# Filler matmuls and a new division of filter copies and products in the first-sequence prologue of a fused FFT-filter and SwiGLU kernel

## The chip, the cores and the metric

One core of one Trainium2 chip. Times are device microseconds (us) of one execution; a profiled execution also has a span, which is 1.8 us shorter than its time (about 2.0 in two kernels). "Clock" is the granted tensor-engine clock as a share of full speed. In the profile's views PE is the tensor engine, PEld its weight loads, DVE VectorE, ACT ScalarE, POOL GpSimd, and SP the engine whose queue issues most transfers.

## The reference

```python
def _attn_ref(x, filt_r, filt_i):            # x (8, 3008, 256), filters (1505, 256)
    X = np.fft.rfft(x, axis=1)
    Y = X * (filt_r + 1j * filt_i)[None]
    return np.fft.irfft(Y, n=x.shape[1], axis=1)

def _moe_ref(x, w_gate, w_val, w_out, rms_g):  # 24064 tokens, 256 -> 1536 -> 256
    xn = x / np.sqrt(np.mean(x * x, axis=-1, keepdims=True) + 1e-06) * rms_g
    g = xn @ w_gate
    return (g / (1 + np.exp(-g)) * (xn @ w_val)) @ w_out
```

## The kernel before

The transform of length 3008 = 47 x 64 is done as matrix products. Eight sequences pass through; the first has a path of its own (the *prologue*), because nothing can run beside it: load x, transform, transpose, multiply by the filter, transform back, transpose, norm, first gate product. From then on one long *loop* of gate, value and output products runs, and the transforms of the later sequences are woven into it.

The filter stands in memory once, but the products need it on both halves of the partitions, so a copy makes the other half. Where these copies ran, before:

```python
def f_dup(c):                       # other half of filter chunk c (4 chunks)
    for t, a, e in ((fr[c], HALF, 0), (fi[c], 0, HALF)):
        if c == 2 or (c == 3 and a):
            nc.scalar.activation(out=t[a:a + HALF], in_=t[e:e + HALF], func=AXT.Copy)
        else:
            nc.gpsimd.tensor_copy(out=t[a:a + HALF], in_=t[e:e + HALF])
```

A *unit* `b_unit(0, i)` is a pair of forward products into PSUM and two filter products (`ss` or `sg`, then `s2`) on VectorE, or, for units 4, 8 and 11, a ScalarE copy `v` out of PSUM and two products on GpSimd. The prologue from the transposes on:

```python
for i in range(8):
    t1_unit(i)                      # 8 transposes + a tile copy
f_dup(0); f_load(3, filt_i, ...); f_dup(1)
for i in range(16):
    if i == 7: f_dup(3)
    b_unit(0, i)
    if i % 2 and i >= 5:
        bit_unit(i - 5)             # inverse products, then copies into gT
        bit_unit(i - 4)
    if i == 4: f_dup(2)
    if i == 11: w_load(0); w_load(1)
...                                 # t2_unit: transposes of gT; norm; scaling
```

For sequence 1, stores and a broadcast load share the in-order SP queue, and the norm's scaling `xn_unit` sits on GpSimd in a fixed slot after the load:

```python
def g_store(b, c):
    nc.sync.dma_start(g_d[b, 4 * c:4 * c + 4, :, :]..., st[b]["t3"].pop(c))
def rho_load(b, m):                 # waits for the small store r_tmp<-rho
    nc.sync.dma_start(rb[:, 0:w], r_d[b, m, 0:w].partition_broadcast(P))
...
# steps: q_unit, rho_load, xn_unit at slots s1 + r
norm_plan(b, m, n_at[m], n_at[m] + step, (2, 6, 10) if b > 1 else (2, 5, 8))
```

## Time and profile before

| | us |
|---|---|
| median of 3 runs | 904.34 (903.84 to 907.87) |
| profiled run: time, span | 903.62, 901.8 |
| first filter product of unit 0 on VectorE | 24.69 |
| last filter product: VectorE, GpSimd | ends 43.41, 41.49 |
| last copy into gT | ends 44.75 |
| first gate output (start of the first Silu) | 52.71 |
| from there to the end ("the loop") | 849.09 |

The landmarks split the span into parts. The last two rows add up to the span. The line of the first gate output (start, duration, engine and line of the kernel, operation, and in brackets what was waited for):

```profile
52.71 0.60 ACT L436 ACTIVATE sg<-pg 128x512 f16<-128x512 f32 x1 [0.23 <-PE pg L432]
```

The other lines that carry this table are in the prediction; the important reading there is the table of stretches, where the clock is 0.67 in the middle of the prologue and 1.00 in the loop.

### The profile page before, as it was taken

Reading aid. Unit: us, or ns where it says so; the run is one execution under the profiler, and the core shown is the slowest. Engines: PE = TensorE matmul, PEld = TensorE weight load, DVE = VectorE, ACT = ScalarE, POOL = GpSimd, SP = SyncE. Lnnn points to the kernel's source line nnn. Section 1 sums busy time; section 2 is a strip of 40 time slices with the busy share of each in tenths; the row PEclk is TensorE's granted clock in tenths of the full one; section 3 lists DMA queues with packets and bytes.
Section 4 is the critical chain, followed back from the end, with each engine's and each line's share of the span. In section 5 each row is a group of like instructions: output and inputs, shape, how many; then the busy total and the mean of one; then the engine's idle time right before and its main releaser. Section 6 shows DMA issues by size and latency. Waiting matters only on the chain.

```text
span 901.8 us, 17407 instructions
## 1 busy us (share of the span) xinstructions
PE 877.6 (97%) x6244; PEld 563.8 (63%) x6244; DVE 678.5 (75%) x1088; ACT 621.4 (69%) x1060; POOL 430.1 (48%) x387
## 2 busy tenths in 40 slices
PE   7789999899999999999999999999999999999997
PEld 5665666666666666666666666666666666666556
DVE  7856767788887887888778886887878887555555
ACT  7667656677777776887667776787657765676444
POOL 6942730455535671477425672377515662145300
PEclk9699999999999999999999999999999999999999
DMA  9395634674655347444654346242262232222201
GB/s 197 71 194 162 144 75 164 155 169 87 170 152 132 68 97 198 118 95 95 141 153 98 95 103 164 95 116 83 83 176 71 66 81 60 93 65 47 72 24 48
DMA packets 79907, 100.91 MB, mean 112 GB/s; under 512 B 8128, under 2 KB 56512, under 8 KB 79436
## 3 DMA queue, kind: packets, MB, share of 16 engines
q1 hardware_dynamic: 69356, 83.32, 34.0%
q0 software_dynamic: 10384, 16.35, 11.4%
q8 instruction: 49, 0.80, 0.4%
q14 instruction: 38, 0.31, 0.1%
q10 hardware_dynamic: 80, 0.13, 0.1%
HBM read 67.67 MB, written 46.78 MB: 127 GB/s over the span
## 4 chain that ended last, share of the span: by engine, by line
PE 83%; issue 6%; DMA 5%; POOL 2%; DVE 2%; ACT 2%; SPq 0%; POOLq 0%; ACTq 0%
PE po L451 24%; PE pg L432 24%; PE pv L432 24%; PE psi L286 3%; PE psb L241 2%; DMA fr<-in_filt_r_dram 2%; PE psn L318 2%; PE psa L204 2%; DMA rb<-r_tmp 1%; DMA g_tmp<-t 1%; DVE o L458 1%; PE psq L347 1%; DVE hh L437 1%; DMA r_tmp<-rho 0%; POOL xc L189 0%
## 5 line engine op out<-in xcount | busy, mean ns | idle before, releaser
L437 DVE TENSOR_TENSOR hh<-pv,sg 128x512 f16<-128x512 f32 (+2 forms) x588 | 393.1, 669 | 200.1 <-ACT sg L436 88.8
L436 ACT ACTIVATE sg<-pg 128x512 f16<-128x512 f32 (+2 forms) x588 | 340.8, 580 | 227.3 <-PE pg L432 217.7
L451 PE MATMUL po<-wo,hh 128*128 128x256 f16 x2244 | 342.9, 272 | 2.8 <-DVE o L458 1.9
L432 PE MATMUL pg<-xn,wg 128*128 128x512 f16 (+2 forms) x1176 | 339.8, 370 | 0.0
L432 PE MATMUL pv<-xn,wv 128*128 128x512 f16 (+2 forms) x1176 | 339.7, 370 | 0.0
L451 PEld LDWEIGHTS <-hh 128*128 128x128 f16 x2256 | 216.4, 98 | 97.4 <-issue 3.8
L277 POOL TENSOR_TENSOR s<-s,s 128x512 f16<-128x512 f16 x96 | 111.0, 1156 | 225.3 <-DVE s L271 150.5
L432 PEld LDWEIGHTS <-wv 128*128 128x128 f16 x1176 | 114.9, 98 | 129.1 <-issue 0.6
L411 POOL TENSOR_TENSOR xn<-y,rb 128x1024 f16<-128x1024 f32 (+1 forms) x45 | 126.1, 2803 | 49.8 <-DMA rb<-r_tmp 36.2
L432 PEld LDWEIGHTS <-wg 128*128 128x128 f16 x1176 | 111.4, 98 | 12.6 <-issue 0.3
L353 POOL TENSOR_TENSOR rho<-u,mhalf 128x4 f32<-128x4 f32 (+1 forms) x48 | 48.9, 1019 | 71.8 <-DVE u L351 71.4
L291 ACT ACTIVATE t<-psi 96x512 f16<-96x512 f32 x112 | 66.3, 592 | 12.6 <-PE psi L286 6.4
L324 ACT ACTIVATE y<-psn,gsb 128x512 f32<-128x512 f32 (+1 forms) x94 | 63.8, 678 | 9.4 <-PE psn L318 2.3
L271 DVE TENSOR_TENSOR s<-psb,fi 64x512 f16<-64x512 f32 x96 | 65.7, 684 | 3.0
L273 DVE SCALAR_TENSOR_TENSOR s<-psb,fi 64x512 f16<-64x512 f32 x96 | 66.5, 693 | 1.3
L247 DVE TENSOR_TENSOR s<-psb,fr 128x512 f16<-128x512 f32 x96 | 65.3, 680 | 0.0
L330 ACT ACTIVATE sq<-psn 128x512 f16<-128x512 f32 (+1 forms) x94 | 54.8, 583 | 0.0
L338 POOL TENSOR_TENSOR sq<-sq 128x512 f16<-128x512 f16 (+1 forms) x34 | 38.5, 1131 | 32.8 <-ACT sq L330 32.7
L209 ACT ACTIVATE t<-psa 128x512 f16<-128x512 f32 x70 | 41.8, 597 | 5.6 <-PE psa L204 2.4
L286 PE MATMUL psi<-s,wi 128*128 128x256 f16 x248 | 45.4, 273 | 0.0
L241 PE MATMUL psb<-t,wb 96*128 96x256 f16 x224 | 43.0, 272 | 1.4 <-DVE s L264 0.9
L286 PEld LDWEIGHTS <-wi 128*128 128x128 f16 x248 | 24.3, 98 | 27.1 <-issue 2.0
(102 smaller groups left out, 544.9 us busy)
## 6 DMA issues: line engine op xcount, KB each, us to landing
out_dram<-o SPq DMA_DIRECT2D x83, 256.0 KB
xc<-in_x_dram POOLq DMA_DIRECT2D x56, 192.0 KB, 6.2
z_tmp<-t SPq DMA_DIRECT2D x28, 384.0 KB
t<-z_tmp SPq DMA_DIRECT2D x28, 384.0 KB
g_tmp<-t SPq DMA_DIRECT2D x56, 192.0 KB
rb<-r_tmp SPq DMA_DIRECT2D x41, 256.0 KB
t<-g_tmp SPq DMA_DIRECT2D x21, 384.0 KB
t<-g_tmp SPq DMA_DIRECT2D x7, 320.0 KB
```

Source lines behind the costliest of these rows:

```text
L247: nc.vector.tensor_tensor(out=s1, in0=ps, in1=f1, op=ALU.mult)
L271: nc.vector.tensor_tensor(out=s2[a], in0=ps[e], in1=f2[e], op=ALU.mult)
L273: nc.vector.scalar_tensor_tensor(out=s2[a], in0=ps[e], scalar=-1.0, in1=f2[e], op0=ALU.mult, op1=ALU.mult)
L277: nc.gpsimd.tensor_tensor(out=s, in0=s1, in1=s2, op=ALU.add)
L286: nc.tensor.matmul(ps[:, u, :], wi_at(q, 2 * i + u), ss[q][:, u, :], start=(q == 0), stop=(q == n - 1))
L291: nc.scalar.activation(out=st[b]["t3"][c][:, 2 * r:2 * r + 2, :], in_=ps[0:KR], func=AXT.Copy)
L324: nc.scalar.activation(out=y[:, dh, 0:w], in_=ps[:, 0:w], func=AXT.Identity, scale=gsb[:, dh:dh + 1])
L411: nc.gpsimd.tensor_tensor(out=xv, in0=yv, in1=rv.unsqueeze(1).to_broadcast([P, 2, n, P]), op=ALU.mult)
L432: nc.tensor.matmul(ps[:, 0:w], wt[:, dt_, ts(jt, P)], xn[:, dt_, :], start=(dt_ == 0), stop=(dt_ == 1))
L436: nc.scalar.activation(out=sg[:, 0:w], in_=pg[:, 0:w], func=AXT.Silu)
L437: nc.vector.tensor_tensor(out=hh[:, 0:w], in0=pv[:, 0:w], in1=sg[:, 0:w], op=ALU.mult)
L451: nc.tensor.matmul(po[s4 // per][:, s4 % per, :], hh[:, ts(s4, P)], wo[:, jt, :], start=(jt == 0 and s4 % per == 0), stop=(jt == JT - 1 an ...
```

## The change

Its intent is to shorten the prologue in two ways. *Fillers*: 63 matmuls on zeros, whose results nobody reads, are put where the tensor engine would wait; they are meant to keep the clock up. *Division of work*: the copies of filter halves go to ScalarE, GpSimd and one transfer; GpSimd takes four units (3, 7, 10, 13) rather than three; six of the eight transpose groups come after the forward products of units 0 to 3 instead of ahead of them, four of them between filter products; small pieces of the tail move to ScalarE.

```diff
+    def b_mm(b, i):
+        ps = bank(3 if b else (0, 3, 4, 5)[i % 4], "psb")...
+        if b == 0 and i > 3:
+            nc.tensor.matmul(ps[:, 0, :], wz[:, 0:P], wz[:, 0:D], start=True, stop=True)
...
-        if (i in (5, 8, 11, 14)) if b else (i in (4, 8, 11)):
+        if (i in (5, 8, 11, 14)) if b else (i in (3, 7, 10, 13)):
...
     def y_first(y, pss, dh):
+        if dh:
+            nc.scalar.activation(out=y[:, dh, :], in_=pss[dh], func=AXT.Identity, ...)
+            return
...
+    def keep_warm(n):
+        o = st[0]["g"][1][:, 4 * KR:512]
+        for _ in range(n):
+            nc.tensor.matmul(o, wz[:, 0:P], wz[:, 0:P], start=True, stop=True)
...
         for m in range(6):
+            if m == 4:
+                warm_up(6, 0)
...
-        for i in range(8):
-            t1_unit(i)
-        f_dup(0)
-        f_load(3, filt_i, fi[3], HALF, nc.gpsimd)
-        f_dup(1)
+        A, G, S = nc.scalar, nc.gpsimd, nc.sync
+        t1_unit(0)
+        t1_unit(1)
+        ps0 = [b_mm(0, i) for i in range(4)]
+        t1_unit(2)
+        t1_unit(3)
+        f_dup(0, 0, A)          # chunk, part (0 real, 1 imaginary), engine
+        f_dup(0, 1, G)
+        f_dup(1, 1, G)
+        f_dup(3, 0, S)
         for i in range(16):
-            if i == 7:
-                f_dup(3)
-            b_unit(0, i)
+            if i == 5:
+                f_dup(2, 1, G)
+            b_unit(0, i, ps0[i] if i < 4 else None)
+            if i == 0:
+                t1_unit(4)
+                t1_unit(5)
+            elif i == 1:
+                t1_unit(6)
+                t1_unit(7)
+            elif i == 3:
+                f_dup(1, 0, A)
+            elif i == 7:
+                f_dup(2, 0, A)
+            elif i == 10:
+                f_dup(3, 1, A)
             if i % 2 and i >= 5:
                 bit_unit(i - 5)
+                keep_warm(4)
                 bit_unit(i - 4)
-            if i == 4:
-                f_dup(2)
-            if i == 11:
+            if i == 13:
                 w_load(0)
                 w_load(1)
         for i in range(12, 16):
             bit_unit(i)
+            if i % 2 == 0:
+                keep_warm(4)
+        warm_up(2, 0)
         t2_unit(0, 1)
...
         first = n_first()
+        warm_up(4, 0)
+        y_first(*first, 1)
         q_unit(0, 0)
+        warm_up(3, 0)
         y_first(*first, 0)
         scale_split(0, 0)
-        y_first(*first, 1)
-        t2_unit(2, 1)
+        t2_unit(2, 0)
         t2_unit(3, 0)
+        warm_up(3, 0)
         scale_apply(0, 0, 3)
+        warm_up(1, 0)
```

The cuts leave out the new signatures of `f_load` and `f_dup`, other PSUM banks for the transposes, and the order of the first loads.

More of the change, by code (lines that the diff above doesn't have):

```diff
@@ L36 @@
 KC = 8
-FC = (8, 8, 8, 8)
 def _make_tables():
@@ L165 @@
     wi = glob.tile([P, 2, K2, P], FP16)
-    fr = [glob.tile([P, n, D], FP32, name="fr%d" % c) for c, n in enumerate(FC)]
-    fi = [glob.tile([P, n, D], FP32, name="fi%d" % c) for c, n in enumerate(FC)]
+    fr = [glob.tile([P, KC, D], FP32, name="fr%d" % c) for c in range(K2 // KC)]
+    fi = [glob.tile([P, KC, D], FP32, name="fi%d" % c) for c in range(K2 // KC)]
     wg = glob.tile([P, 2, DFF], FP16)
@@ L227, in wi_at @@
         return wi[:, q, k, :] if k else tb[:, 3 + q, :]
-    def b_unit(b, i):
-        if b:
-            ps = bank(3, "psb")
-        else:
-            ps = bank((0, 3, 4, 5)[i % 4], "psb")
-        ps = ps.rearrange("p (a d) -> p a d", a=2)
+    def b_mm(b, i):
+        ps = bank(3 if b else (0, 3, 4, 5)[i % 4], "psb").rearrange("p (a d) -> p a d", a=2)
+        if b == 0 and i > 3:
+            nc.tensor.matmul(ps[:, 0, :], wz[:, 0:P], wz[:, 0:D], start=True, stop=True)
         for u in range(2):
@@ L241, in b_unit @@
             nc.tensor.matmul(ps[:, u, :], w[:, k, :], t, start=True, stop=True)
+        return ps
+    def b_unit(b, i, ps=None):
+        if ps is None:
+            ps = b_mm(b, i)
         f1, f2 = filt(2 * i, 2)
@@ L379, in y_first @@
     def y_first(y, pss, dh):
+        if dh:
+            nc.scalar.activation(out=y[:, dh, :], in_=pss[dh], func=AXT.Identity, scale=gsb[:, dh:dh + 1])
+            return
         nc.vector.tensor_scalar(out=y[:, dh, :], in0=pss[dh], scalar1=gsb[:, dh:dh + 1],
@@ L483, in o_store, with f_load @@
             nc.sync.dma_start(prev[:, H - 1, :], o3[64:P, 3, :])
-    NC = K2 // KC
     def raw(src, row, ap):
         return bass.AP(tensor=src.tensor, offset=src.offset + row * D, ap=ap)
-    def f_load(c, src, t, p0, eng):
+    def f_load(c, e, eng):
         lo = 1 if c == 0 else 0
+        src, t, p0 = ((filt_r, fr[c], 0), (filt_i, fi[c], HALF))[e]
         eng.dma_start(t[p0 + 16:p0 + 63:2, :, :].rearrange("p a d -> p (a d)"),
@@ L500, in f_load, with f_dup @@
             eng.dma_start(t[p0 + 1:p0 + 48:2, 0, :], raw(src, 32, [[64 * D, 24], [1, D]]))
-    def f_dup(c):
-        for t, a, e in ((fr[c], HALF, 0), (fi[c], 0, HALF)):
-            if c == 2 or (c == 3 and a):
-                nc.scalar.activation(out=t[a:a + HALF], in_=t[e:e + HALF], func=AXT.Copy)
-            else:
-                nc.gpsimd.tensor_copy(out=t[a:a + HALF], in_=t[e:e + HALF])
+    def f_dup(c, e, eng):
+        t = (fr, fi)[e][c]
+        a, o = (0, HALF) if e else (HALF, 0)
+        if eng is nc.scalar:
+            eng.activation(out=t[a:a + HALF], in_=t[o:o + HALF], func=AXT.Copy)
+        elif eng is nc.sync:
+            eng.dma_start(t[a:a + HALF], t[o:o + HALF])
+        else:
+            eng.tensor_copy(out=t[a:a + HALF], in_=t[o:o + HALF])
     def at_unit(m, dh):
@@ L528, in t1_unit @@
         st[0]["t2"][g] = dst
-        pool, tag = ((psO, "po0"), (psO, "po1"), (psM, "mx"), (psB, "mb"))[g % 4]
+        pool, tag = ((psG, "pg"), (psV, "pv"))[g % 2]
         ps = pool.tile([P, 4, D], FP16, tag=tag, name="pt1")
@@ L536, in t1_unit @@
                 nc.tensor.transpose(ps[:, a, ts(dh, P)], src, ident)
-        if g % 2 == 0 or g == 7:
+        if g not in (1, 4):
             nc.vector.tensor_copy(out=dst, in_=ps[0:KR])
@@ L626 @@
         nc.sync.dma_start(wbp, tab["wbp"])
-        for c in range(NXC):
-            x_load(0, c)
         def zero(t):
@@ L632, in zero @@
                                  in_=mhalf[0:HALF, 0:1].to_broadcast([HALF, KC * D]), func=AXT.Copy, scale=0.0)
+        for c in range(NXC):
+            x_load(0, c)
         nc.gpsimd.memset(fr[0][0:HALF], 0.0)
@@ L642 @@
             zero(fi[c][HALF:P])
-        for c in range(4):
-            f_load(c, filt_r, fr[c], 0, nc.sync)
-            if c < 3:
-                f_load(c, filt_i, fi[c], HALF, nc.gpsimd)
         with nc.allow_non_contiguous_dma(reason="one gain a partition"):
             nc.sync.dma_start(gsb, moe_rms_g.rearrange("(a p) -> p a", p=P))
+        for c in range(4):
+            f_load(c, 0, nc.sync)
+            f_load(c, 1, nc.gpsimd if c < 3 else nc.sync)
         warm_up(14, 1)
```

## The prediction

> **What bounds the kernel now.** I read the page's busy shares first, then busy time by stretch to see where the tensor engine is not full, then the chain that ended last from 0 to 56 us, and last the vector engine's and GpSimd's timelines of that part.
>
> ```profile
> PE 877.6 (97%) x6244; PEld 563.8 (63%) x6244; DVE 678.5 (75%) x1088; ACT 621.4 (69%) x1060; POOL 430.1 (48%) x387
> ```
>
> ```profile
> 0.00:23.90 23.90, 19.20 (x219) 13.82 (x220) 17.04 (x27) 18.18 (x22) 16.43 (x27) 0.93 0.89 195
> 23.90:44.60 20.70, 15.70 (x161) 12.12 (x159) 17.29 (x29) 13.56 (x22) 19.42 (x18) 0.67 0.32 63
> 44.60:52.70 8.10, 6.08 (x53) 4.26 (x54) 4.01 (x10) 3.36 (x6) 5.74 (x9) 0.80 1.21 176
> 52.70:901.80 849.10, 836.66 (x5813) 533.63 (x5811) 640.16 (x1024) 586.25 (x1011) 388.53 (x336) 1.00 0.44 110
> ```
>
> The columns are stretch, length, then busy us (and instructions) of PE, PEld, DVE, ACT and POOL, the granted clock, DMA share and GB/s. From 52.7 us, when the first gate product is ready, the tensor engine is busy 836.66 of 849.10 us at full clock. The diff touches nothing after that point: each function it edits keeps its old path for every later sequence. So all that can move is the first 52.7 us: load, forward transform and transposes to 23.9, filter products of the first sequence to 44.6, then transpose, norm and first gate product. In the middle stretch POOL is busy 19.42 and DVE 17.29 of 20.70 us, while the clock is 0.67: the products and filter copies bound it, not matmul work. The chain says the same:
>
> ```profile
> 17.60 10.79 DMA fr<-in_filt_r_dram
> ...
> 28.50 1.92 ACT fr L505
> ...
> 37.77 1.27 POOL ss L264
> ...
> 42.47 2.13 ACT gT L559 x5
> ...
> 50.77 1.01 PE pt L570 x8
> ```
>
> The filter's rows come from memory, a copy makes their other half, products wait, and at the end a short serial tail runs. The vector engine's timeline gives the waits:
>
> ```profile
> 24.69 0.69 DVE L263 TENSOR_TENSOR ss<-psb,fr 128x512 f16<-128x512 f32 x1
> 31.00 0.69 DVE L264 TENSOR_TENSOR hh<-psb,fi 128x512 f16<-128x512 f32 x1 [0.63 <-POOL fi L507]
> 37.86 0.69 DVE L263 TENSOR_TENSOR ss<-psb,fr 128x512 f16<-128x512 f32 x1 [1.11 <-POOL ss L263]
> 40.93 0.69 DVE L263 TENSOR_TENSOR ss<-psb,fr 128x512 f16<-128x512 f32 x1 [0.58 <-PE psb L241]
> 42.73 0.68 DVE L264 TENSOR_TENSOR hh<-psb,fi 128x512 f16<-128x512 f32 x1
> ```
>
> The 26 products start 0.60 us apart, 15.6 us of work, spread from 24.69 to 43.41 = 18.7 us: about 3 us are waits. GpSimd's copies, and the clock where it sags, complete the picture:
>
> ```profile
> 21.59 1.92 POOL L507 COPY fr<-fr 64x2048 f32<-64x2048 f32 x1 [1.68 <-DMA fr<-in_filt_r_dram]
> 23.57 1.89 POOL L507 COPY fi<-fi 64x2048 f32<-64x2048 f32 x1
> ```
>
> ```profile
> 15.20:18.60 3.40, 1.42 (x18) 1.15 (x19) 1.75 (x3) 1.33 (x3) 1.67 (x3) 1.00 0.74 168
> 18.60:22.00 3.40, 3.40 (x35) 3.40 (x34) 1.38 (x2) 1.20 (x2) 0.97 (x3) 0.51 0.87 209
> 25.40:28.80 3.40, 1.86 (x25) 1.13 (x22) 3.31 (x6) 0.90 (x2) 3.36 (x5) 1.00 0.89 176
> 28.80:32.20 3.40, 2.60 (x24) 1.99 (x22) 2.77 (x5) 3.38 (x2) 3.25 (x3) 0.52 0.25 48
> 45.80:49.20 3.40, 1.88 (x25) 1.31 (x24) 0.83 (x2) 1.99 (x4) 1.04 (x2) 1.00 1.12 154
> 49.20:52.60 3.40, 2.96 (x19) 2.09 (x20) 2.61 (x6) 1.12 (x3) 3.40 (x7) 0.53 1.29 190
> ```
>
> Each 3.4 us stretch with the tensor engine busy under about 1.9 us is followed by one at half clock.
>
> **What the Trainium skill says.** "TensorE: Matmul & The Clock Gate", Part 1, says a free-running window of 3413 ns decides between half and full clock. The trace agrees: the clock changes near 18.65, 22.05, 28.9, 42.5, 49.3 and 52.7 us, all multiples of 3.4 us apart. "GPSIMD Engine Reference", section 1, gives GpSimd no PSUM access; the trace shows it as a 0.60 us ScalarE copy (v) ahead of each GpSimd unit. "DMA: Bandwidth & Descriptors", Anatomy of one DMA, fits 2.0 us + bytes / 436 GB/s. For the new 524 KB copy that gives 3.2 us, an estimate; no transfer of this trace shows it alone.
>
> **The change part by part.** I lay the new order out by hand, each engine in its own program order, with this trace's durations.
>
> *Start of the products.* Six fillers (512 columns) fall into the idle before 16.51, when the last x piece lands, so they delay nothing; they should spare the half clock from 18.65 to 22.05. Units 0 to 3 get their forward products after two of eight transposes, about 20.6. What then releases unit 0 is the filter. GpSimd's copy of fr waited for its rows to 21.59; no byte of that load moves. The fr copy goes to ScalarE, 21.5 to 23.4 (1.91 us), beside GpSimd's fi copy (1.89 us), where before the two ran in a row to 25.46. Unit 0 starts at 23.45 instead of 24.69: 1.2 us earlier.
>
> *Vector engine.* Twelve units instead of 13: 24 x 0.60 = 14.4 us; three transposed tiles are now copied between units 0 and 2, 3 x 0.60 = 1.8. From 23.45 that ends at 39.65 if nothing waits.
>
> *ScalarE.* Four filter copies at 1.91, four v copies at 0.60, seven pairs of gT copies at 0.85, one tile copy at 1.02: 17.0 us. Placed in order: fr0 to 23.4, tile to 24.4, v3 to 24.95, fr1 to 26.9, gT pair, v7 from 29.65 (its forward product waits behind unit 2's bank, free at 28.85), fr2 to 32.1 (rows landed at 28.4; unit 8 wants it at 32.45, just in time), two gT pairs to 33.8, v10 to 34.4, fi3 to 36.3 (unit 12's turn is at 36.05), gT to 37.15, v13 to 37.7.
>
> *GpSimd.* Three copies and four units of two 1.26 us products, 15.8 us. fi1 ends at 25.4; unit 3 runs 25.4 to 27.9, fi2 to 29.8, unit 7 30.25 to 32.75, unit 10 34.4 to 36.9, unit 13 37.75 to 40.25. Unit 13 is then last: its inverse products at 40.3, units 14 and 15 to 41.7, last gT copies to 42.2. Before they ended at 44.60. This step is worth 2.4 us.
>
> *The transfer.* fr3's other half goes through the queue after its rows, which land by about 30; 3.2 us later is 33 to 34, against a use at 36. The rows of fi3 follow fr3 on the same queue; DMA was idle from about 30 to 42, so this hides.
>
> *Fillers.* In all 63: 32 of 128 columns, 12 of 256, 19 of 512. At full clock a 512-column product takes 0.216 us (pairs of gate products start 0.43 apart), so these are about 32 x 0.055 + 12 x 0.11 + 19 x 0.216 = 7.2 us of PE time. It stands where PE waits, so it adds little. In the tail one group is in the way: six large fillers and eight transposes queue between the norm sum and the broadcast product, which I put at 0.1 us late.
>
> *Tail, from last gT copy to first gate output.* Now 52.71 - 44.60 = 8.11 us. The broadcast product and the gate pair ran at half clock (1.12 and 1.09 us of pipe where full clock shows 0.61 and 0.59), and a gain product (0.74) and a tile copy (0.41) stood on the vector engine before the last scaling. Those two move to ScalarE. Placed again: norm sum ends +3.35, broadcast product +5.75, scaling to +7.1, gate output +7.55. So 0.55 us less.
>
> Sum: 2.4 + 0.55 = 2.95 us. The first gate output comes at 49.75, and the loop's 849 us follow unchanged: 904.34 - 2.95 = 901.4. I allow a little for a start less throttled than drawn and set 901.3.
>
> **Rivals.** First, fillers fail: the stretch after the transposes (about 25 to 29) may still lie below what keeps the clock. A pair of units with fillers is then 1.56 us of PE at full clock, 3.1 at half, above the 2.4 us that two vector units take, so PE becomes the bound for a window or more. The pass is then 1 to 3 us worse: 902 to 904. Speaking for it: stretches with PE busy 2.6 us at half clock stayed there. Against: with fillers I count some 2.8 of 3.4 us, and stretches with 2.9 kept full clock. Second, ScalarE's order becomes the bound: v7, fr2, v10, fi3 and v13 wait in one line, and each us lost there reaches unit 13. All slack there is under 0.5 us; this would give 902 to 903. Third, weights: their loads follow unit 13 on GpSimd's queue, at 40.3 instead of 41.4, so they gain 1.1 us where their reader gains 3. The first landed 5.4 to 6.7 us after issue, so by 48.3; the first gate product wants wg and wv at about 49: hidden, with 1 to 2 us spare. Fourth, my start could be pessimistic (vector units packed better, second throttle gone): 899.5 to 900.5.
>
> **Range and chances.** The rivals lie between 899.5 and 904, and medians of the old kernel's runs scatter by 0.5 us with one at 907.87. Eight in ten: 899.6 to 903.2. Two per cent is 18 us, a third of the whole prologue; no rival reaches it. Faster by over 2%: 0.01; within: 0.985; slower: 0.005.
>
> **What would show it right or wrong.** Unit 0's first vector product at 23.4 to 23.6, waiting for ScalarE's fr copy; last gT copies near 42.2; first gate output near 49.75; granted clock 1.00 from 7 us on; 849 us from there to the end. Wrong if the first gate output moves but the end does not (a later DMA wait takes it back), if the clock shows 0.5 between 28 and 42, or if unit 13 on GpSimd ends much after 40.3.

## The result, and the profile after

After: median 898.46 us of 4 runs (897.98 to 900.15); before, with one more run beside it: 904.49. Ratios in this document are the mean time of one kernel's runs over that of the other's of the same rounds, so not quite the ratio of the quoted medians. Here it is 0.9929 (0.9901 to 0.9957): within 2%, as expected, but a gain of 6.0 us, twice the 2.95 predicted, and 1.1 us below the range.

The page's first part, after:

```profile
PE 877.4 (98%) x6307; PEld 563.0 (63%) x6307; DVE 676.7 (75%) x1085; ACT 624.0 (70%) x1063; POOL 427.2 (48%) x384
```

PE has 63 more instructions, all fillers, and is no busier. The stretches, after, in the columns that the prediction explains:

```profile
0.00:23.90 23.90, 19.67 (x219) 13.06 (x220) 16.78 (x27) 18.61 (x22) 16.08 (x26) 1.00 0.89 200
23.90:44.60 20.70, 16.32 (x235) 13.28 (x234) 16.96 (x29) 15.47 (x25) 17.94 (x16) 1.00 0.47 92
44.60:52.70 8.10, 7.77 (x67) 4.79 (x65) 4.09 (x10) 6.01 (x12) 5.68 (x9) 1.00 1.25 185
```

The clock is 1.00 throughout, against 0.93, 0.67 and 0.80. Work has moved from GpSimd (19.42 to 17.94 in the middle stretch) to ScalarE (13.56 to 15.47). The chain of waits up to 56 us (start, length, what) now begins with x and not with the filter:

```profile
5.36 11.66 DMA xc<-in_x_dram
...
19.04 1.19 PE pt L543 x15
...
39.19 1.26 POOL hh L266
...
48.11 1.30 DVE xn L405 x2
```

The timelines of VectorE, ScalarE and GpSimd after, a line from each (start, duration, and what is waited for):

```profile
23.66 0.68 DVE L265 TENSOR_TENSOR ss<-psb,fr 128x512 f16<-128x512 f32 x1
```

```profile
49.86 0.60 ACT L441 ACTIVATE sg<-pg 128x512 f16<-128x512 f32 x1 [0.19 <-PE pg L437]
```

```profile
39.19 1.25 POOL L266 TENSOR_TENSOR hh<-v,fi 128x512 f16<-128x512 f32 x1
```

They give the landmarks against the prediction:

| us | before | predicted | after |
|---|---|---|---|
| unit 0 starts | 24.69 | 23.45 | 23.66 |
| last VectorE product ends | 43.41 | 39.65 | 39.88 |
| last GpSimd product ends | 41.49 | 40.25 | 40.44 |
| last copy into gT by ScalarE ends | 44.60 | 42.2 | 42.32 |
| first gate output | 52.71 | 49.75 | 49.86 |
| loop, from there to the end | 849.09 | 849.09 | 847.04 |

So the hand-laid order held to 0.25 us at every landmark of the prologue: 2.85 us gained of 2.95 predicted. But the loop, which no line of the diff touches, was 2.05 us shorter. These two make the 4.9 us between the two profiled runs (903.62 and 898.71). The last 1.1 us is where the medians lie: before's profiled run was 0.9 us under its median, after's 0.25 us above. The question for the experiments was therefore: did the change shorten the loop too, or did two samples fall on different sides of a scatter?

### The profile page after: what moved, and what is told of

It is laid out like the page before. It is cut to its first block, busy times and chain, and to the rows that moved or that the text cites. A ratio compares the mean times of both kernels' runs of the same rounds, so it can differ in the third digit from the quotient of the medians. Undisturbed runs are those within 1.5% of the kernel's fastest.

```text
span 896.9 us, 17537 instructions
## 1 busy us (share of the span) xinstructions
PE 877.4 (98%) x6307; PEld 563.0 (63%) x6307; DVE 676.7 (75%) x1085; ACT 624.0 (70%) x1063; POOL 427.2 (48%) x384
## 4 chain that ended last, share of the span: by engine, by line
PE 87%; issue 5%; DVE 3%; DMA 2%; POOL 2%; ACT 1%; POOLq 0%; DVEq 0%; ACTq 0%; SPq 0%
PE po L456 25%; PE pg L437 25%; PE pv L437 25%; PE psi L288 3%; PE psb L238 3%; PE psn L320 2%; PE psa L203 2%; DMA xc<-in_x_dram 1%; DMA rb<-r_tmp 1%; DVE o L463 1%; PE psq L349 1%; DVE hh L442 1%; PE pt L543 0%; POOL xc L188 0%; PE pt L582 0%
```

## The experiments

All sixteen runs came in four jobs of four; those of one job share a chip and the runs of the kernel before. The landmarks are of each run's one profile, the times of all its runs. All outputs are right.

| run | first gate output | loop | median (n) | mean clock | ratio to before (95%) |
|---|---|---|---|---|---|
| r_before | 52.67 | 848.63 | 903.73 (6) | 0.989 | 0.9983 (0.9957-1.0009) |
| r_after | 49.88 | 849.82 | 900.54 (6) | 0.999 | 0.9945 (0.9920-0.9969) |
| no_fill | 50.76 | 849.94 | 903.17 (4) | 0.991 | 0.9970 (0.9934-1.0007) |
| tail_only | 52.88 | 848.32 | 903.10 (4) | 0.991 | 0.9983 (0.9951-1.0015) |
| late_loop | 52.09 | 847.41 | 901.87 (4) | 0.999 | 0.9983 (0.9967-0.9999) |
| fill_only | 49.94 | 851.26 | 902.33 (4) | 0.997 | 0.9981 (0.9964-0.9998) |
| three_pool | 50.35 | 847.75 | 900.66 (4) | 0.997 | 0.9976 (0.9949-1.0004) |
| old_copies | 51.66 | 847.74 | 901.24 (4) | 0.998 | 0.9975 (0.9959-0.9991) |
| r_after2 | 49.64 | 849.36 | 900.81 (6) | 0.997 | 0.9971 (0.9946-0.9995) |
| g_act | 50.18 | 847.32 | 899.48 (6) | 0.999 | 0.9959 (0.9938-0.9981) |
| xn_late | 50.39 | 845.51 | 897.59 (6) | 0.997 | 0.9945 (0.9919-0.9972) |
| g_act_xn | 52.35 | 845.35 | 897.54 (6) | 0.997 | 0.9943 (0.9920-0.9966) |
| before_fix | 50.76 | 847.44 | 900.22 (6) | 0.991 | 0.9966 (0.9946-0.9987) |
| after_fix | 49.12 | 845.38 | 896.85 (6) | 0.999 | 0.9928 (0.9910-0.9947) |
| fill_fix | 53.39 | 846.51 | 900.13 (6) | 0.997 | 0.9964 (0.9944-0.9984) |
| nofill_fix | 52.44 | 845.56 | 899.77 (6) | 0.990 | 0.9961 (0.9943-0.9980) |

### The pair again, and two parts alone

r_before and r_after are the two kernels without an edit.

> The kernel before, unchanged, as a control. 'Loop' is the time from the first gate output to the end of the span: 849.1 us in the first profile of before, 847.0 in that of after, where I had predicted no difference. Theory N (the extra gain is scatter of transfer landings from execution to execution): first gate output again at 52.7 +- 0.1, loop between 848.3 and 850.5, off the first profile by more than 0.3. Theory S (systematic): first gate output 52.7, loop 849.1 +- 0.15 again, waits at the same places. Median time 904.5.

> The changed kernel, unchanged, as a control. Theory N: first gate output 49.9 +- 0.1, loop between 847.0 and 848.7 and different from the first profile. Theory S: loop 847.0 +- 0.15. Median time 898.5, 6.0 us below before in the same rounds; under N rather 4.5 to 5.5.

The prologue came out as before (52.67 and 49.88: 2.8 us), though in r_before unit 0 started at 22.08 and not at 24.69. But after's loop was now 849.82 us, longer than before's 848.63. The medians differ by 3.2 us in these 6 runs each; against all 11 runs of before of the job, by 4.3. In the original rounds it was 6.0, and it is 2.2 in the third job. So the loop has no fixed time, and its 2.05 us are not simply the change's. How much of them recurs is seen only when the loop is cut into pieces, further down.

no_fill is after with every filler taken out (the expectation says 49 in one place; it is all 63).

```diff
-        if b == 0 and i > 3:
-            nc.tensor.matmul(ps[:, 0, :], wz[:, 0:P], wz[:, 0:D], start=True, stop=True)
...
-                keep_warm(4)
...
-        warm_up(4, 0)
```

> The changed kernel without any of its 49 added fillers in and between the products and in the tail and x wait (all 63 out). Theory 'fillers only repair the clock, the reordering gives most': clock falls to 0.5 for most of 18 to 42 us, first gate output at 50.5 to 51.3, time 899.5 to 900.5. Theory 'fillers give most of it': first gate output at 52 or later, time 901.5 or more.

tail_only is before with after's tail: the last fillers, and the gain product and the tile copy on ScalarE.

```diff
         for i in range(12, 16):
             bit_unit(i)
+            if i % 2 == 0:
+                keep_warm(4)
+        warm_up(2, 0)
...
+        warm_up(4, 0)
+        y_first(*first, 1)
...
-        y_first(*first, 1)
-        t2_unit(2, 1)
+        t2_unit(2, 0)
```

> The kernel before with only the tail of the change (from the last inverse products to the loop: fillers, gain product and tile copies on ScalarE). My tail step says 0.55 us, plus 0.3 us that the loop's first products lost to the half clock: first gate output 52.1 to 52.2, time 903.5 to 903.8. If the fillers are in the way it is 904.5 or more.

In tail_only's profile the way from the last gT copy (45.49) to the first gate output (52.88) took 7.39 us against 7.96 in before (52.71 - 44.75): the tail's 0.55 us is there. (Its first gate output is later than the 52.1 to 52.2 expected, because unit 0 started at 25.10.) Its median is 0.6 under r_before's, well inside the interval. no_fill's profile kept full clock from 18 to 40 us without any filler (it fell at 40.11 and again at 46.94) and still had its first gate output 0.9 us after the filled kernel; its runs had a mean clock of 0.991 and lay between 900.2 and 904.1. Neither is enough to divide a gain of 3 us, because the loop scatters by as much.

### Does a later start lengthen the loop, and what is each part worth beside the others?

late_loop tests the rival that the loop is short because it starts early: 13 fillers of 512 columns push its start back.

```diff
         t2_unit(5, 0)
+        warm_up(13, 0)
         w_load(2)
```

> The changed kernel with 13 more large fillers (2.8 us at full clock) just before the loop, so that the loop starts when it did before. Theory P (the loop is shorter because it starts earlier against the transfers): first gate output near 52.6, loop back to 849, time 903.3. Theories N and 'clock': loop 847.0 to 848, time 901.2 to 901.9.

The first gate output came 2.2 us later (52.09), near before's place, and the loop stayed at 847.41. A late start alone does not make the loop long. (The added fillers kept full clock; a start at half clock is not tested by this run.)

fill_only is before with all 63 fillers at the corresponding places and nothing else.

```diff
+        if b == 0 and i > 3:
+            nc.tensor.matmul(ps[:, 0, :], wz[:, 0:P], wz[:, 0:D], start=True, stop=True)
...
                 bit_unit(i - 5)
+                keep_warm(4)
                 bit_unit(i - 4)
```

> The kernel before with all 63 fillers and nothing moved. If products and copies bound the stage, last gT copy at 44.3 to 44.6, only the tail gains: first gate output 52.0 to 52.3, time 903.5. If half clock on the products was itself costly, first gate output 51.3 or earlier, time 902.5 or less.

three_pool is after with before's three GpSimd units.

```diff
-        if (i in (5, 8, 11, 14)) if b else (i in (3, 7, 10, 13)):
+        if (i in (5, 8, 11, 14)) if b else (i in (4, 8, 11)):
...
-            if i == 13:
+            if i == 11:
                 w_load(0)
```

> The changed kernel with units 4, 8 and 11 on GpSimd as before instead of 3, 7, 10 and 13. The vector engine then carries 13 units: 23.66 + 15.6 + 1.8 = 41.1 without waits, against 40.44 for GpSimd's last unit now, but only unit 15 remains behind it. Theory 'GpSimd's late unit 13 sets the end': last gT copy 41.9 to 42.3, time 898.0 to 898.5. Theory 'the fourth unit is worth a unit of vector time (1.2 us)': last gT copy 43 to 43.5, time 899.2 to 899.7.

old_copies is after with before's places for the filter copies.

```diff
-        f_dup(0, 0, A)
+        f_dup(0, 0, G)
         f_dup(0, 1, G)
+        f_dup(1, 0, G)
         f_dup(1, 1, G)
-        f_dup(3, 0, S)
         for i in range(16):
-            if i == 5:
-                f_dup(2, 1, G)
+            if i == 7:
+                f_dup(3, 0, A)
+                f_dup(3, 1, G)
...
-            elif i == 3:
-                f_dup(1, 0, A)
-            elif i == 7:
+            elif i == 4:
                 f_dup(2, 0, A)
-            elif i == 10:
-                f_dup(3, 1, A)
+                f_dup(2, 1, A)
```

> The changed kernel with the filter copies on the engines and in the places of before (the later fi3 load stays on the sync queue). By my step unit 0 starts 1.2 to 1.9 us later (its fi copy is GpSimd's second: 25.4) and GpSimd holds 5 copies and 4 units. Last gT copy 44 to 46, time 900.5 to 902.5. If the copies' place does not matter: last gT copy 42.3, time 898.5.

The profiles separate the parts: in after, the last gT copy came 18.81 us after unit 0's start (42.47 - 23.66), and in r_after and r_after2 18.82. In three_pool it was 19.89 (42.96 - 23.07), in old_copies 21.13 (44.27 - 23.14). With the fillers in, the filter copies' places are thus worth 2.3 us and the fourth GpSimd unit 1.1 us of that distance. The two were not undone together, unit 0 itself started about half a microsecond earlier in both profiles, and in both the clock of the middle stretch was 0.92 and not 1.00 (half clock for one stretch of 3.4 us), so these distances hold a part of the clock's cost too. The times do not resolve this: the four medians of the job span 1.7 us. fill_only was the surprise: its prologue was as short as after's (49.94) in its profile, yet its loop took 851.26 us, the longest of all.

I cut the loop at VectorE's copies of the finished output tiles and compared the pieces over all profiles. Two pieces differ most: the one around 115 us, between the second and the third output (place A), and the one around 175 us (place B). Place A was 2.25 us longer in fill_only than in the shortest, 0.75 in before, 0 in after. Place B was 1.7 to 2.2 us longer in every kernel so far than it proved it could be, and 3.89 in r_after.

The same cut shows a part of the loop's difference that does recur. The piece from the first gate output to the first output tile was 0.28 us over its shortest in before and 0.92 in r_before, and at most 0.01 in after and r_after: before enters the loop with the clock at half (r_before up to 54.17 us), after does not. Two more pieces near the end are 0.23 us longer each in every profile with the old tail, and in none with the new one; why is not known. With places A and B set to their shortest, the loop is 846.5 us in before and 846.9 in r_before, against 845.2 and 845.4 in after and r_after. So a little over 1 us of the loop's gain comes with the change, and the rest of the 2.05 us is scatter.

Place A, in the waits of the SP queue of before between 90 and 124 us (line, what it waits for: total us, count, longest us):

```profile
SPq L362 <- DMA r_tmp<-rho: 13.4, 2, 7.3
```

The SP queue works in order. Twice it stands, 6.1 and 7.3 us, at `rho_load`, whose source is the small store of `rho`; the two stores landed 1.7 and 5.4 us after their issue, and the rest of the wait is for the norm's sum ahead of them. The stores of sequence 1 stand behind it, and ScalarE's next copy needs the buffer that such a store frees. Before's ScalarE timeline there:

```profile
115.34 0.59 ACT L291 ACTIVATE t<-psi 96x512 f16<-96x512 f32 x1 [1.15 <-DMA g_tmp<-t]
```

ScalarE waited 1.15 us for a store to land; in fill_only it was 2.64. Its copies for the tensor engine come late, the tensor engine idles, and the clock drops: 0.74 in fill_only from 114 to 117 us and 0.69 from 117 to 120.

Place B, the tensor engine's timeline of r_after, with 2.05 us of waiting for GpSimd's sum `s`:

```profile
175.51 0.27 PE L288 MATMUL psi<-s,tb 128*128 128x256 f16 x1 [2.05 <-POOL s L279]
176.78 1.06 PE L437 MATMUL pv<-xn,wv 128*128 128x512 f16 x2
```

and of after, where the same wait was 1.68:

```profile
174.63 0.27 PE L288 MATMUL psi<-s,tb 128*128 128x256 f16 x1 [1.68 <-POOL s L279]
175.72 0.59 PE L437 MATMUL pv<-xn,wv 128*128 128x512 f16 x2
```

In r_after the pair of value products then took 1.06 us instead of 0.59: half clock. A stretch table from 174 to 178 us says the same, 0.80 in r_after and 1.00 in after. The length of the wait does not decide this alone: in late_loop and three_pool it was 2.00 and 2.01 us, and the clock stayed full. In r_after the clock steps down at 176.39, and PE was busy 1.36 us of the 3.41 before that; in after, in the stretch of the same phase (172.82 to 176.23), 1.73. What GpSimd stood at in r_after, from its timeline:

```profile
171.49 2.86 POOL L416 TENSOR_TENSOR xn<-y,rb 128x1024 f16<-128x1024 f32 x1 [3.51 <-DMA rb<-r_tmp]
```

It waited 3.51 us for the broadcast row of the norm, then scaled for 2.86 us, and only then came to the sums that the inverse products need.

### Taking the two waits out of the loop

Neither place has to do with the change, but both decide what a measurement of it shows. So the third job takes each away, without loosening any dependence: another queue for one, a later slot for the other. r_after2 is after once more.

> The changed kernel again, beside the next three on the same chip. The loop (first gate output to end) has come out between 847.0 and 849.8 for it. What I now hold: two places of the loop wait for landings, at output copies 1 to 2 (a store of the second sequence's inverse products stands behind a load that waits for a small store) and 5 to 6 (GpSimd waits for the same kind of load); each costs 0.1 to 0.9 us, and 1 to 2 us more where the wait leaves a clock window below its mark. First gate output 49.9; excess over the shortest seen, in those two stretches together, 0.1 to 2.7 us. Median 899 to 900.5.

g_act puts the stores of sequence 1 on ScalarE's queue, so that they do not stand behind the broadcast load.

```diff
     def g_store(b, c):
-        nc.sync.dma_start(g_d[b, ...]..., st[b]["t3"].pop(c))
+        (nc.scalar if b == 1 else nc.sync).dma_start(g_d[b, ...]..., st[b]["t3"].pop(c))
```

> The changed kernel with the second sequence's eight stores issued from ScalarE's queue, so that they no longer stand behind the load that waits 7 to 8 us. If that order is the cause, the excess at copies 1 to 2 is under 0.1 us and no half clock shows near 115 us; median 0.3 to 0.8 us below r_after2. If the landing itself is slow whatever the queue, the excess stays between 0 and 2 us, and eight issues of about 0.5 us on ScalarE may even add to it.

xn_late gives GpSimd's scaling of two tiles of sequence 1 a later slot, so that the row has landed.

```diff
-                          (2, 6, 10) if b > 1 else (2, 5, 8))
+                          (2, 6, 10) if b > 1 else (2, 5, 11 if m in (1, 2) else 8))
```

> The changed kernel with two scaling steps of the second sequence three slots later, so that GpSimd does not stand waiting for their broadcast rows with the third sequence's additions behind it. If that is the cause, the tensor engine's wait of 1.7 us near 172 us is gone or under 0.7 us and copies 5 to 6 take 19.0 to 20.1 us instead of 20.1 to 22.3; median 0.5 to 1.7 us below r_after2. If not, the wait stays at 1.7.

g_act_xn has both edits.

> Both together. If the two places are separate their gains add: loop 845.5 to 847 in every profile, median 897.5 to 899, and less scatter between runs than r_after2. If the loop's scatter has other causes, the spread stays at 2 us or more.

Place B is settled. In xn_late's GpSimd timeline the scaling comes after the sum and waits for nothing:

```profile
169.93 1.14 POOL L279 TENSOR_TENSOR s<-s,s 128x512 f16<-128x512 f16 x1 [1.92 <-DVE s L273]
171.04 2.86 POOL L416 TENSOR_TENSOR xn<-y,rb 128x1024 f16<-128x1024 f32 x1
```

The piece at place B fell by 1.7 us or more and was the shortest seen in all six kernels with this edit; the loop came to 845.5 us and 845.4. The two medians are 897.59 and 897.54, 3.2 us under r_after2 of the same job (2.5 by the means). The expectation that g_act_xn would scatter less was not met: the standard deviation of its six runs is 2.14 us, of r_after2's 2.40.

Place A is less certain. r_after2 had 2.02 us there and g_act none, and g_act's median is 1.3 us lower (by the means 1.0, with a standard deviation of 2 us in each). But xn_late without the store edit also had none in its profile, nor had after, late_loop, three_pool and old_copies, so that the 2 us come and go by themselves. The order of the queue is seen in the trace; that the edit cures the place is likely, not shown.

g_act_xn's prologue was late (52.35) because x landed at 17.98 us in that profile and the transposes ran at half clock: the prologue scatters too.

### The change measured with a quiet loop

The last job puts both loop edits into four kernels: before, after, before with fillers, and after without fillers. after_fix is g_act_xn once more.

```diff
# the same two edits in all four
+        (nc.scalar if b == 1 else nc.sync).dma_start(...)
+                          (2, 6, 10) if b > 1 else (2, 5, 11 if m in (1, 2) else 8))
```

> The kernel before with both loop edits (second sequence's stores on ScalarE's queue, two scaling steps three slots later). The two waits are taken out of the loop of both kernels, so before_fix against after_fix measures the change itself with less scatter. Theory 'the change acts on the prologue alone': loop 845.2 to 846.5 here too, first gate output 52.5 to 53, and the difference of the medians to after_fix 2.5 to 3.7 us. Theory 'the change also shortens the loop': loop here 847 or more, difference 4.5 to 6.

> The changed kernel with both loop edits, again. Prologue alone: first gate output at 49.6 to 50.4 (later only where the x piece lands late), loop 845.2 to 846.2, median 897 to 898.

> The kernel before with all 63 fillers and both loop edits. In its profile without the loop edits the fillers alone had the first gate output at 49.94, all of the gain. If fillers alone really give nearly all, median within 0.7 us of after_fix. By my own parts (0.55 us for fillers and tail) it would be 2 us or more above after_fix.

> The changed kernel without fillers, with both loop edits. In its profile without the loop edits the reordering alone had the first gate output at 50.76. If reordering alone gives most, median 0.7 to 1.5 us above after_fix. If the clock then falls in most executions and costs more than that one profile showed, 2 us or more above, with clock 0.986 to 0.995.

The standard deviation of six runs fell to 0.65 us for before_fix and 0.66 for after_fix, where it was 1.60 for r_before and 1.04 and 2.40 for the two repeats of after. The edits are not shown to be the reason: the 11 runs of before in this job have 1.80 us, but g_act_xn, the same kernel as after_fix, had 2.14 on the chip of the third job. Still, within this job the change can be read from the times: 900.22 to 896.85, so 3.4 us by the medians and by the means (3.2 by the spans). Fillers alone: 900.22 to 900.13, 0.1 us. All the rest without fillers: 900.22 to 899.77, 0.45 us. The two parts alone make 0.55 us, together 3.4.

The profiles, cut at the landmarks, do not show a gain of the prologue alone:

| us | unit 0 starts | from there to the last gT copy | from there to the first gate output | loop |
|---|---|---|---|---|
| before_fix | 22.99 | 19.81 | 7.96 | 847.44 |
| after_fix | 22.91 | 18.81 | 7.40 | 845.38 |
| fill_fix | 23.27 | 22.50 | 7.62 | 846.51 |
| nofill_fix | 25.66 | 18.78 | 8.00 | 845.56 |

In before_fix the first gate output came at 50.76, 2 us earlier than in before, but its loop was 2.06 us longer than after_fix's. That is what its expectation had named for "the change also shortens the loop" (847 or more), with a difference of the medians that it had named for the other theory. The view from its first gate output on (columns as in the prediction's stretches) shows half clock for 3.2 us:

```profile
50.76:53.96 3.20, 3.20 (x15) 1.68 (x14) 1.02 (x2) 1.54 (x3) 2.29 (x5) 0.50 1.24 190
```

The loop's first piece was 1.36 us longer there than in after_fix, whose clock was full. So the change gains in the prologue and at the loop's start, and one profile divides the sum differently from the next.

The stretch from 23.90 to 44.60 of the four profiles, in the order before_fix, after_fix, fill_fix, nofill_fix:

```profile
23.90:44.60 20.70, 14.24 (x171) 10.86 (x170) 15.99 (x27) 14.08 (x23) 18.30 (x17) 0.84 0.41 76
```

```profile
23.90:44.60 20.70, 16.25 (x226) 12.71 (x224) 16.21 (x28) 15.43 (x25) 18.11 (x16) 1.00 0.54 102
```

```profile
23.90:44.60 20.70, 16.64 (x190) 13.84 (x189) 15.32 (x26) 12.62 (x20) 17.52 (x16) 0.75 0.36 70
```

```profile
23.90:44.60 20.70, 15.84 (x203) 13.46 (x201) 18.08 (x30) 15.71 (x24) 15.79 (x13) 0.83 0.40 83
```

Of these four only the kernel with both parts has clock 1.00. The fillers without the new order did not hold it in this profile. VectorE's timeline of fill_fix shows a wait for GpSimd that they don't cover:

```profile
37.52 0.69 DVE L265 TENSOR_TENSOR ss<-psb,fr 128x512 f16<-128x512 f32 x1 [2.98 <-POOL ss L265]
```

VectorE stands there 2.98 us; in before_fix the same wait was 1.90. Whether the clock held also divides fill_fix's six runs: the three with a mean clock of 0.998 or more took 898.89 to 899.31 us, the three from 0.994 to 0.997 took 900.95 to 901.88. Fillers alone gained about 1.3 us on before_fix when the clock held and lost about 1 us when it did not. So its profile (53.39 for the first gate output) is a bad sample and fill_only's (49.94) a good one, and the 0.1 us is the mean of both kinds.

The new order without fillers falls to 0.83 as well, but its middle stretch did not suffer: 18.78 us, as in after_fix, and VectorE's filter products wait for nothing in its timeline. What nofill_fix lost in this profile lies before and after. Unit 0 came 2.75 us later: the last piece of x landed at 17.53 us, after 2.63 us of waiting, and from 17.03 to 23.86 the tensor engine ran at half clock. The tail took 8.00 us instead of 7.40. So the two parts need each other by the six times of each kernel, and in these profiles the losses come with half clock, at a different place in each; the single waits were not taken out one by one, so that this is the likely reason and not a shown one.

after_fix is also the fastest version by its median: 896.85 us (896.26 to 898.22), ratio 0.9928 to before in its job; the lowest run of the changed kernel itself was 897.98.

## Why the prediction was right or wrong

**Right: the prologue's order.** The placement of copies and units on each engine, step by step from the durations of before, gave every landmark to within 0.25 us. "First gate output at 49.75" was 49.86, and the predicted 2.95 us compares with 2.85 between the two profiles. There is luck in how the sum divides: the 1.2 us of an earlier unit 0 exist only against this one profile of before. In r_before (22.08) and before_fix (22.99) unit 0 started before after's 23.66, and the copies and units took longer instead (22.67 and 19.81 us from there to the last gT copy, where before took 20.06 and after 18.81).

**Wrong: "the loop's 849 us follow unchanged".** This step failed. The loop's instructions are the same, but its time is not a constant: from 847.04 to 851.26 us over the profiles without the loop edits. Two things stand in its place. The first is scatter: place A cost from 0 to 2.25 us and place B about 2 us, in r_after 3.9, and not by kernel, so that the plain means of three profiles each agree, 848.7 (before, r_before, tail_only; and after, r_after, r_after2). The second belongs to the change: "the diff touches nothing after that point" is true of the code, not of the clock with which the loop starts. Its first piece was 0.28, 0.92 and 1.36 us over the shortest in before, r_before and before_fix, and at most 0.01 in after's profiles; with places A and B set to their shortest, before's loops (846.5, 846.9, 847.4) are 1.0 to 2.3 us longer than after's (845.2 to 845.4). The prediction had no term for this, although its own window from 49.20 to 52.60 shows half clock up to the loop's start. The recorded after was a low draw, with a loop 2.3 to 2.8 us under those of its own repeats, whose medians are 900.54 and 900.81. Pooled over all jobs, before has a mean of 904.0 (50 runs) and after 900.2 (16 runs), so 3.8 us (in the first two pairs of profiles 2.8 us from the prologue and a little over 1 from the loop). 901.3 would have been about 1 us high.

**Wrong: the range.** "Medians of the old kernel's runs scatter by 0.5 us" was read from three runs, of which one lay 3.5 us off and was set aside as a single case. Same-job differences of this one pair came out as 6.0, 4.3 and 2.2 us. A range of 1.7 us downward for a result taken from a handful of runs was too narrow; the loop's scatter of some 2 us either way had to be in it.

**Partly wrong: what the parts are worth.** The sum "2.4 + 0.55", order on one side, tail and clock on the other, fell. The tail's 0.55 was confirmed at 0.57 in tail_only. But the 2.4 us are not the order's own: without fillers it gives 0.45 in all. "The products and filter copies bound it, not matmul work" held for the new order even at a clock of 0.83 (18.78 us in nofill_fix) but not for the old one, whose distance from unit 0 to the last gT copy was 22.67 us at clock 0.59 (r_before) and 19.44 at 1.00 (fill_only). The sentence that fillers stand "where PE waits, so it adds little" counted what they cost; what they give, at the transposes, in the tail and at the loop's start, was only in part in the sum.

**Wrong, but small: what releases unit 0.** "What then releases unit 0 is the filter" and "waiting for ScalarE's fr copy": ScalarE's fr copy ended at 23.24, and after's chain goes from x through the transposes, while VectorE's two tile copies ended just before unit 0, at 23.66 instead of 23.45. That the two times are so near is luck. Over the profiles with after's order it lay from 22.91 to 26.15, set by when x landed and which clock the transposes had.

**The rivals.** "Fillers fail" was not seen in after, but it was near. Its clock steps at 5.57 and at 896.45 us, 261 times 3.413 us apart, and this gives the place of the windows between. The quietest is

```profile
26.05:29.46 3.41, 1.68 (x26) 1.50 (x26) 3.41 (x7) 1.76 (x3) 3.35 (x3) 1.00 0.74 159
```

PE was busy 1.68 us of it, less than the "about 1.9 us" of the prediction, and full clock followed; in three_pool the window from 27.54, with 1.71, was followed by half clock. The prediction's rule fitted before but has no sharp edge. "ScalarE's order becomes the bound" and "weights" were not seen: the first gate product waits for no weights, and GpSimd's waits for ScalarE's copies v, 1.53 us before unit 10 and 0.66 before unit 13, were in the hand-laid order (1.65 and 0.85). The pessimistic-start rival (899.5 to 900.5) named the repeats' medians nearly right, for another cause. The 3.2 us for the new transfer of fr3 rested on a fit that "DMA: Bandwidth & Descriptors", Anatomy of one DMA, gives for transfers issued by GpSimd, and this one goes out from the SP queue; its landing is not on record, but VectorE's product with it (unit 12, at 36.21) waited for nothing.

**Open.** How often each place in the loop costs its 2 us; why two pieces near the end are 0.23 us longer with the old tail; whether the store edit cures place A; and what the runs of 902 to 905 us are that most groups of after's kinds still have one of, and before's of 907 and more, none of which was profiled.

## What to carry to other kernels

Before a gain of three microseconds is read off one pair, time the same pair again on another chip and compare the part that the edit does not touch. If that part differs between two profiles, cut it into pieces and see which differences recur: here some were scatter, and some were the edit's after all, carried over by the clock. Where such a part stands in in-order queues behind small round trips, take those waits out first; here this was worth about as much as the change. Fillers and a better order can be worth little alone and much together: here 0.1 and 0.45 us alone, 3.4 us together.

## What the Trainium skill lacked or had wrong

- "TensorE: Matmul & The Clock Gate", HAM oscillation, gives as its abstract rule that gaps above about 3.4 us lower the clock; the section after it names frequent short idles as a second case without a figure. No fall here followed a gap of that length. With windows of 3.413 us laid from the first clock step of each of the 18 traces, the clock fell 22 times before the kernel's end, each time after a window in which PE was busy 1.15 to 2.25 us and never idle for more than 2.14 us on end. After more than 2.25 us busy it never fell; between 1.63 and 2.25 both happened (1.68 in after kept the clock, 1.71 in three_pool did not). The ends of matmuls are modelled in these traces, so the edge may be sharper than this. The page gives no share of busy time for a window.
- The same page, Part 4 (PE-mode transpose), says that full clock does not engage for transposes, which do not count as busy in the same way. In after, the 48 transposes from 21.92 took 3.04 us on the chain, 0.063 us each, with the granted clock at 1.00. In the window from 22.63 to 26.05 PE was busy 2.81 us, only 0.49 of them without these transposes, and full clock followed; no window with so little work kept it. So here they counted.
- "DMA: Bandwidth & Descriptors", Anatomy of one DMA, puts a small transfer at 2.0 us plus bytes over 436 GB/s. The two `rho` stores at place A in before took 1.7 us (2.0 KB) and 5.4 us (1.5 KB) from issue to landing: the smaller one nearly three times the fit, with other transfers under way. The page does say that a semaphore wait happens on the issuing sequencer before dispatch; it doesn't draw a consequence that shows here, that every later store in the same engine's program order stands behind such a wait (13.4 us in two waits of SP; ScalarE waited 1.15 us in before and 2.64 us in fill_only).
- No page says that two executions of one program may differ by 2.8 us long after the start (847.04 and 849.82 us for one loop), nor how many runs a difference of 0.3% needs: six of each with a standard deviation of 0.65 us were enough, six with 2.4 us were not.
